# Softmax sums of four head pairs in one burst behind a projection, inverses spread through a DRAM scratch

## The chip, the cores and the metric

The kernel runs on one core of one Trainium2 chip. The metric is the device time of one execution in microseconds (us), the median of several runs. The core has five engines with a queue each: TensorE (PE in the profile, with its weight loads as PEld), VectorE (DVE), ScalarE (ACT), GpSimd (POOL) and SyncE (SP). Here POOL issues the loads, and SP the stores, the DMA transposes and the small copies inside the chip. Matrix products land in PSUM, which has eight banks of 128 partitions by 512 fp32; VectorE and ScalarE carry them on to SBUF.

## What is computed

A linear attention (keys and values are projected from 1024 positions to 64) followed by a two-layer network with a squared relu. There are 8 batches, 8 heads, 1024 positions and a head width of 64; the network goes from 512 to 2048 and back to 512.

```python
k_proj = np.einsum('ks,bhsd->bhkd', E, k)
v_proj = np.einsum('ks,bhsd->bhkd', F, v)
attn = np.exp(scale * np.matmul(q, k_proj.transpose(0, 1, 3, 2)))   # less the row maximum
attn = attn / (np.sum(attn, axis=-1, keepdims=True) + 1e-09)
x = np.matmul(attn, v_proj)         # heads side by side: 8192 tokens x 512
h = np.maximum(x @ w_in, 0.0)
out = h * h @ w_out
```

## The kernel before

**The network.** A batch is two chunks of 512 tokens. Both products of the network are done by a seven-product scheme on 2x2 blocks (sums and differences of blocks are formed on VectorE), so each has seven half-size products where eight would be plain. `Group` (lines 647 to 713) is the first product: a chunk has four groups, and a group has seven products p1, p5, p4 (of the group before), p6, p2, p3, p7, each of four matmuls of 256 columns (line 665). Their results are copied on ScalarE (L557, L690), passed through relu on ScalarE (L675) or added and passed through relu on VectorE (L679), and squared (L154). `second_spread` (line 590) is the second product, cut into quarters of four matmuls (L585). Its results leave through `put` (L575 on ScalarE or L154 on VectorE, then the store L579); `keep` (L557) puts a partial result aside in one of five buffers named "u".

**The order of the work.** TensorE's order is written out by hand. From the second batch on, the loop `both()` goes step by step: one product of the first layer and one quarter of the second, eight matmuls in all. A batch has 56 steps. The attention of a later batch is put between steps: `at(step, ...)` and `on(step, batch, name)` enter it in a plan. In the loop that fills the plan, t = 56(b-1)+28 is counted for batch b, and the attention entered is that of batches b+1 and b+2. The other engines' orders are made by a scheduler from the dependencies; SP and POOL take their transfers in order, so one that waits holds back those behind it.

**The attention of one batch.** `project` (L270, L271) projects all heads of K and V in 16 matmuls of 512 columns, two at a time, into the pair of banks that the attention has (one pair from the second batch on): K into the lower 64 partitions of the first bank, V into the upper 64 of the second. The other halves stay free. `keep_k` (L258, L259) and `keep_v` (L263, L264) copy them out. DMA transposes make kT (L304) and qT (L331). `scores` (L339) takes one pair of heads, and `exponentials` (L353) its Exp, into one of four buffers. `sums_spread` (L392) takes two pairs of heads: eight matmuls with a stationary operand of ones, 64 rows by 32 columns each, sum the exponentials over keys, each sum repeated on 32 partitions. Ln (L396) and Exp with scale -1 (L397) on 128x1024 make the inverse, and eight copies from SBUF to SBUF on SP (L403) spread it to the 64 rows of each head, 128 KB each. `values` (L415) multiplies with V, and VectorE (L419) multiplies by the inverse.

At the end, `second_seven` (line 624) is the second product of the last chunk. Its last product is accumulated in one bank, and its two halves leave by ScalarE (L575) and VectorE (L573) on two queues.

Of the kernel before, what the change touches and what calls it, by code (L numbers as in the profile page):

```python
# [1 line left out]

# [7 lines left out]
P = 128  # L10
F32 = mybir.dt.float32
BF16 = mybir.dt.bfloat16
AF = mybir.ActivationFunctionType
# [6 lines left out]
def kernel(  # L20
# [11 lines left out]
    nc = tc.nc  # L32
# [31 lines left out]
    part_pool = ctx.enter_context(tc.tile_pool(name="part", bufs=5))  # L64
    out_pool = ctx.enter_context(tc.tile_pool(name="outp", bufs=3))
    psum = ctx.enter_context(tc.tile_pool(name="ps", bufs=1, space=bass.MemoryType.PSUM))
    turn = {"att": 0, "bank": 0, "step": 1, "pairs": 2}

    lent = ctx.enter_context(ExitStack())
# [5 lines left out]
    def att_psum(shape=(P, 2, TCH), dtype=F32):  # L75
        turn["att"] += 1
        return pair_psum(turn["att"] % turn["pairs"], shape, dtype)

    def bank(shape=(P, 512), dtype=F32, n=None):
        if n is None:  # L80
            turn["bank"] += turn["step"]
            n = turn["bank"]
        return psum.tile(list(shape), dtype, tag=f"bank{n % 4}", name="ps_bank")
# [111 lines left out]
    def w_out_form(n, fb):  # L195
        if n in (1, 2, 3):
            return w_out_blk(fb + (0 if n == 1 else HF))[:, HM if n == 3 else 0:DM if n == 3 else HM]
        return w_out_sum[:, {5: 0, 6: 1, 7: 2, 4: 3}[n], fb]
# [28 lines left out]
    for h in half:  # L227
        nc.scalar.copy(kp[:, h].rearrange("p h a d -> p (h a d)"), zeros[:])
    kT = const_pool.tile([P, H, 2, KP], BF16, name="kT")
    VALUE_QUADS = ((LO, 0, 0, LO), (HI, 1, 1, HI), (HI, 0, 1, LO), (LO, 1, 0, HI))  # L230

    class Attention:
# [30 lines left out]
            nc.scalar.copy(self.vp[HI], view)  # L263
            nc.vector.tensor_copy(self.vp[LO], view)  # L264

        def project(self):
            ps = att_psum()
            for i in range(NI):
                f, l = i == 0, i == NI - 1
                nc.tensor.matmul(ps[LO, 0], lhsT=ET[:, i, :], rhs=self.K[:, :, i, :], start=f, stop=l)  # L270
                nc.tensor.matmul(ps[HI, 1], lhsT=FT[:, i, :], rhs=self.V[:, :, i, :], start=f, stop=l)  # L271
            self.keep_k(ps[LO, 0], slice(0, H))
            self.keep_v(ps[HI, 1])

        def project_k(self, g):
            ps = bank()
# [50 lines left out]
                    )  # L327
            nc.vector.tensor_copy(self.qT[:, 2 * pr:2 * pr + 2], ps[:])

        def transpose_q_dma(self):  # L330
            nc.sync.dma_start_transpose(  # L331
                self.qT[:].rearrange("p h n t -> p (h n) t"), self.Q[:].rearrange("p h i d -> p (h i d)")
            )


        def scores_mm(self, ps, pr, n):
# [46 lines left out]
                    nc.vector.tensor_copy(rs[j][lack:lack + 32], rs[j][have:have + 32])  # L383
                self.rs[pr + j] = rs[j]

        def sums_spread(self, pr):

            ps = att_psum()
            for j in range(2):
                for o, par, a, r in VALUE_QUADS:  # L390
                    c = 32 * (2 * a + j)
                    nc.tensor.matmul(  # L392
                        ps[c:c + 32, par], lhsT=ones[r, 0:32], rhs=self.e[pr + j][r, a], start=True, stop=True
                    )
            inv = soft_pool.tile([P, 2, TCH], F32, tag="rs", name="inv")
            nc.scalar.activation(inv[:], ps[:], AF.Ln)  # L396
            nc.scalar.activation(inv[:], inv[:], AF.Exp, scale=-1.0)  # L397
            for j in range(2):
                rs = soft_pool.tile([P, 2, TCH], F32, tag="rs", name="rs")
                for a in range(2):  # L400
                    have = 32 * (2 * a + j)
                    for to in (64 * a, 64 * a + 32):
                        nc.sync.dma_start(rs[to:to + 32], inv[have:have + 32])  # L403
                self.rs[pr + j] = rs

        def values(self, pr, spare=False):

# [40 lines left out]
    class Chunk:  # L448
# [104 lines left out]


        def keep(self, ps):
            u = part_pool.tile([P, DM], F32, name="u")
            nc.scalar.copy(u[:], ps)  # L557
            return u

        def half_product(self, n, i, ps, fresh=False):  # L560
            for fb in range(HF):
                nc.tensor.matmul(  # L562
                    ps[:, i * HM:(i + 1) * HM], lhsT=self.h_form(n, fb)[:, i * P:(i + 1) * P],
                    rhs=w_out_form(n, fb), start=fresh and i == 0 and fb == 0, stop=fb == HF - 1,
                    skip_group_check=True,
                )

        def put(self, a, mh, ps, more=None, part=None):
            o = out_pool.tile([P, 2, HM], F32, name="o_sb")
            n = slice(0, 2) if part is None else slice(part, part + 1)  # L570
            ps = ps.rearrange("p (i m) -> p i m", i=2)[:, n]
            if part:
                nc.vector.tensor_copy(o[:, n], ps)  # L573
            elif more is None:
                nc.scalar.copy(o[:, n], ps)  # L575
            else:
                tt(o[:, n], ps, ALU.add, more.rearrange("p (i m) -> p i m", i=2)[:, n])
            i = 4 * self.c + a + 2 * n.start
            (nc.scalar if part == 0 else nc.sync).dma_start(  # L579
                out_tokens[self.b][:, i:i + 2 * (n.stop - n.start) - 1:2, mh * HM:(mh + 1) * HM], o[:, n]  # L580
            )

# [38 lines left out]
            self.put(1, 0, chain)  # L621
            yield

        def second_seven(self, first, chain, other, last=False):
            def product(n, ps, fresh=False):
                self.half_product(n, 0, ps, fresh)
                yield
                self.half_product(n, 1, ps, fresh)

            yield from product(1, first, True)  # L630
            nc.scalar.copy(chain, first)
            yield
            yield from product(5, other, True)
            p5 = self.keep(other)
            yield
            yield from product(6, chain)
            u2 = self.keep(chain)
            yield
            yield from product(2, first)
            self.put(0, 0, first)  # L640
            yield
            yield from product(7, chain)
            self.put(1, 1, chain, p5)
            yield
            yield from product(3, other)
            self.put(0, 1, other, u2)
            yield
            yield from product(4, chain)
            if last:
                self.put(1, 0, chain, part=0)  # L650
                self.put(1, 0, chain, part=1)
            else:
                self.put(1, 0, chain)
            yield

    class Group:

# [63 lines left out]
    with tc.manual_schedule(engines={PE}):  # L721
# [33 lines left out]
        def at(step, fn, *args, **kwargs):  # L755
            plan.setdefault(step, []).append(lambda: fn(*args, **kwargs))

        def run(steps, start=0):
            for step, _ in enumerate(steps, start + 1):
                for stage in plan.pop(step, []):  # L760
                    stage()
            return step
# [62 lines left out]
        def second_bank(n):  # L825
            return second_pool.tile([P, 512], F32, tag=f"second{n}", name="ps_second")
# [40 lines left out]
        def on(step, b, name, *args):  # L867
            at(step, lambda: getattr(atts[b], name)(*args))
# [2 lines left out]
        on(6, 1, "chunk_values", 1, 0)  # L871
        on(12, 1, "chunk_sums", 1, 1)
        on(15, 1, "chunk_values", 1, 1)
        for b in range(B - 1):
            t = 56 * (b - 1) + 28
            if b:
                on(t + 1, b + 1, "scores", 3)
                on(t + 3, b + 1, "sums_spread", 2)
                on(t + 7, b + 1, "values", 0)
                on(t + 10, b + 1, "values", 1)  # L880
                on(t + 20, b + 1, "values", 2)
                on(t + 23, b + 1, "values", 3)
                at(t + 24, lambda b=b: chunk[b + 1, 0].sum_x())
            at(t + 51, lambda b=b: chunk[b + 1, 1].sum_x())
            if b + 2 < B:
                if b:
                    on(t + 11, b + 2, "load_q", lambda b=b: atts[b + 1].done)
                on(t + (26 if b else 32), b + 2, "transpose_q_dma")
                on(t + (28 if b else 36), b + 2, "project")
                on(t + (30 if b else 37), b + 2, "transpose_k_dma")  # L890
                if b + 3 < B:
                    at(t + (32 if b else 37), begin, b + 3)
                    on(t + (32 if b else 37), b + 3, "load_kv", lambda b=b: atts[b + 2].kT_done)
                on(t + (44 if b else 45), b + 2, "scores", 0)
                on(t + (47 if b else 48), b + 2, "scores", 1)
                on(t + (50 if b else 51), b + 2, "sums_spread", 0)
                on(t + (53 if b else 54), b + 2, "scores", 2)
        steps = both()
        run(steps)
        assert not plan, plan  # L900
        run(chunk[B - 1, 1].second_seven(second_bank(0)[:], second_bank(1)[:], bank(n=turn["bank"] + 1)[:], True))


# [28 lines left out]
```

The softmax here doesn't subtract the row's maximum and nothing guards it: scores larger than these inputs give would overflow.

## Time and profile before

| | |
|---|---|
| median of 3 runs | 474.89 us (473.21, 474.89, 474.94) |
| the profiled execution: its time | 473.25 us |
| its span, first to last instruction | 471.5 us |
| granted TensorE clock | 1.000 |
| one batch in the middle (163.15 to 218.50 us) | 55.35 us |
| ScalarE busy in it | 35.60 us |
| VectorE busy in it | 42.98 us |
| transfers `rs<-inv` | 96 of 128 KB, 2.3 us to landing (2.2 to 7.6) |

The profile is of one execution. Busy time of an engine is the time in which an instruction of it runs; matmuls are pipelined and their ends are modelled, so durations of neighbours overlap and starts are the better measure. A row of the timeline gives start, duration, engine, line, operation, tiles, form, how many were merged, and in brackets the idle time ahead and what ended it. A row of the groups gives the number of instructions, then busy time and mean ns of one, then idle time ahead of them.

### The profile page before, as it was taken

What the parts mean: (1) busy time and instruction counts of PE and PEld (TensorE: products, weight loads), DVE (VectorE), ACT (ScalarE), POOL (GpSimd) and SP (SyncE); (2) the same over time, 40 slices, a digit from 0 to 9 for tenths busy, and PEclk for the clock granted to TensorE, in tenths of its full rate; (3) what the DMA queues carried; (4) which work ended last, traced back from release to release, by engine and by line L of the source; (5) the groups of instructions that cost most, each with busy time, mean ns of one, the idle gap of its engine ahead of it and who ended that gap; (6) DMA issues with size and microseconds to landing.
All of it is one profiled execution on the core that took longest, in us unless ns stands there. A gap on an engine that the chain in (4) does not pass through costs nothing.

```text
span 471.5 us, 10107 instructions
## 1 busy us (share of the span) xinstructions
PE 464.1 (98%) x4123; PEld 367.6 (78%) x4141; DVE 347.6 (74%) x595; ACT 297.5 (63%) x484; POOL 34.0 (7%) x47
## 2 busy tenths in 40 slices
PE   8999999999999999999999999999999999999996
PEld 4544677888788787887888888888878878888885
DVE  2469985776968779567895779787796679968571
ACT  4488585887467864677457774568636875555641
POOL 7430100100010000100001000100000000000000
PEclk9999999999999999999999999999999999999999
DMA  9999999895869578785969749695692154101012
GB/s 182 201 205 207 158 206 203 166 217 106 186 138 207 137 141 195 133 171 131 170 180 153 170 98 183 153 197 147 116 219 71 39 132 100 68 24 68 24 69 89
DMA packets 85743, 67.90 MB, mean 144 GB/s; under 512 B 34368, under 2 KB 82240, under 8 KB 85696
## 3 DMA queue, kind: packets, MB, share of 16 engines
q0 software_dynamic: 32208, 29.23, 40.6%
q1 hardware_dynamic: 53344, 37.89, 30.1%
q8 instruction: 32, 0.52, 0.4%
q10 hardware_dynamic: 144, 0.13, 0.1%
q14 instruction: 15, 0.12, 0.1%
HBM read 59.24 MB, written 16.78 MB: 161 GB/s over the span
## 4 chain that ended last, share of the span: by engine, by line
PE 97%; DMA 1%; DVE 1%; ACT 1%; issue 0%; SPq 0%; ACTq 0%; DVEq 0%
PE ps_bank L665 38%; PE ps_second L585 36%; PE ps_bank L502 6%; PE ps_bank L562 3%; PE ps_att L270 3%; PE ps_att L339 2%; PE ps_second L562 2%; PE ps_att L415 2%; DMA k_f<-in_k_dram 1%; PE ps_att L392 1%; PE ps_bank L314 1%; PE ps_att L349 1%; PE ps_att L345 1%; PE ps_bank L220 0%; PE ps_att L289 0%; PE ps_bank L278 0%
## 5 line engine op out<-in xcount | busy, mean ns | idle before, releaser
L154 DVE TENSOR_TENSOR h<-h 128x1024 bf16<-128x1024 bf16 (+1 forms) x170 | 105.4, 645 | 43.9 <-ACT h L675 38.7
L665 PE MATMUL ps_bank<-x_sum,w_in_sum 128*128 128x256 bf16 x672 | 101.1, 273 | 0.1
L665 PEld LDWEIGHTS <-w_in_sum 128*128 128x128 bf16 x896 | 85.5, 98 | 18.9 <-issue 6.3
L585 PEld LDWEIGHTS <-h 128*128 128x128 bf16 x896 | 87.6, 98 | 10.7
L679 DVE CUSTOM_DVE_ANT_0 h<-ps_bank,u 128x512 bf16<-128x512 f32 x112 | 73.8, 685 | 16.2 <-PE ps_bank L665 12.1
L557 ACT COPY u<-ps_bank 128x512 f32<-128x512 f32 x115 | 68.0, 591 | 24.9 <-PE ps_bank L665 23.7
L690 ACT COPY ps_bank<-ps_bank 128x512 f32<-128x512 f32 x56 | 32.0, 571 | 81.5 <-PE ps_bank L665 81.5
L675 ACT ACTIVATE h<-ps_bank 128x512 bf16<-128x512 f32 x112 | 67.9, 607 | 16.7 <-PE ps_bank L665 15.8
L665 PEld LDWEIGHTS <-w_in 128*128 128x128 bf16 x672 | 64.3, 98 | 14.5 <-issue 5.2
L585 PEld LDWEIGHTS <-s 128*128 128x128 bf16 x672 | 65.7, 98 | 7.6
L665 PE MATMUL ps_bank<-xT,w_in 128*128 128x256 bf16 x448 | 67.3, 273 | 0.3
L585 PE MATMUL ps_second<-w_out_sum,s 128*128 128x256 bf16 x448 | 67.2, 273 | 0.0
L585 PE MATMUL ps_second<-w_out_sum,h 128*128 128x256 bf16 x448 | 67.0, 273 | 0.0
L585 PE MATMUL ps_second<-w_out,h 128*128 128x256 bf16 x448 | 64.7, 272 | 0.0
L419 DVE TENSOR_TENSOR xT<-ps_att,rs 128x512 bf16<-128x512 f32 x48 | 30.9, 685 | 13.7 <-PE ps_att L415 13.7
L353 ACT ACTIVATE expT<-ps_att 128x1024 bf16<-128x1024 f32 x32 | 33.1, 1034 | 5.2 <-PE ps_att L339 3.4
L665 PE MATMUL ps_bank<-x_sum,w_in 128*128 128x256 bf16 x224 | 33.7, 273 | 0.3
L665 PE MATMUL ps_bank<-xT,w_in_sum 128*128 128x256 bf16 x224 | 33.6, 273 | 0.1
L154 DVE TENSOR_TENSOR o_sb<-ps_second,u 128x512 f32<-128x512 f32 x29 | 19.9, 685 | 18.7 <-PE ps_second L585 13.6
L585 PE MATMUL ps_second<-w_out,s 128*128 128x256 bf16 x224 | 33.6, 273 | 0.0
L502 PE MATMUL ps_bank<-xT,w_in 128*128 128x512 bf16 x124 | 28.8, 379 | 0.4 <-issue 0.2
L154 DVE TENSOR_TENSOR s<-h 128x1024 bf16<-128x1024 bf16 x32 | 22.0, 691 | 3.7 <-PE ps_second L585 3.0
(97 smaller groups left out, 453.4 us busy)
## 6 DMA issues: line engine op xcount, KB each, us to landing
out_dram<-o_sb SPq DMA_DIRECT2D x63, 256.0 KB, 2.5
rs<-inv SPq DMA_DIRECT2D x96, 128.0 KB, 2.3
K_sb<-in_k_dram POOLq DMA_DIRECT2D x7, 1024.0 KB, 10.2
V_sb<-in_v_dram POOLq DMA_DIRECT2D x7, 1024.0 KB, 14.5
Q_sb<-in_q_dram POOLq DMA_DIRECT2D x6, 1024.0 KB, 11.8
w_out<-in_moe_w_out_dram POOLq DMA_DIRECT2D x4, 512.0 KB, 15.8
Q_sb<-in_q_dram POOLq DMA_DIRECT2D x4, 256.0 KB, 11.0
V_sb<-in_v_dram POOLq DMA_DIRECT2D x2, 512.0 KB, 10.8
```

What stands on the lines that cost most here:

```text
L154: return nc.vector.tensor_tensor(out=o, in0=x, in1=y, op=op)
L270: nc.tensor.matmul(ps[LO, 0], lhsT=ET[:, i, :], rhs=self.K[:, :, i, :], start=f, stop=l)
L353: self.done = nc.scalar.activation(e[:], ps[:], AF.Exp, scale=SCALE)
L419: self.done = nc.vector.tensor_tensor(out=self.xT[:, pr, :, par], in0=ps_x[par].rearrange("p (c t) -> p c t", c=2), in1=rs[:, par].rearran ...
L502: nc.tensor.matmul(ps[:], lhsT=w_in_blk(cb, fb), rhs=self.xT[:, cb, self.c].rearrange("p a t -> p (a t)"), start=(cb == 0), stop=(cb == NC ...
L557: nc.scalar.copy(u[:], ps)
L562: nc.tensor.matmul(ps[:, i * HM:(i + 1) * HM], lhsT=self.h_form(n, fb)[:, i * P:(i + 1) * P], rhs=w_out_form(n, fb), start=fresh and i == ...
L585: nc.tensor.matmul(ps[:, i * HM:(i + 1) * HM], lhsT=self.h_form(n, fb)[:, i * P:(i + 1) * P], rhs=w_out_form(n, fb), start=fresh and i == ...
L665: nc.tensor.matmul(ps[:, j * HC:(j + 1) * HC], lhsT=w_in_form(n, cb, 2 * self.g + j), rhs=self.chunk.x_form(n, cb), start=fresh and j == 0 ...
L675: nc.scalar.activation(self.out(kh, a), ps[:], AF.Relu)
L679: nc.vector._custom_dve(TENSOR_ADD_SAT, out=self.out(kh, a), in0=ps[:], in1=more[:], s0=3.0e38, s1=0.0)
L690: nc.scalar.copy(self.chain[:], self.first[:])
```

## The change

The sums of all four head pairs of a batch are taken in one burst of 16 matmuls. The stationary operand is a new constant `pick`: for pair m, its columns 8m to 8m+7 are ones and the rest zeros, so the four pairs accumulate into one tile of 32 partitions with eight rows each. They go to the half of the attention's two banks that the projection leaves free: in batches 3 to 6 `project` of the batch after runs first and the sums behind it, in batches 2 and 7 the sums run alone. There are one Ln for each bank on 64 partitions, and one Exp on 128x512. The inverses go to a DRAM scratch in two writes. `spread` reads a pair's rows back, each repeated eight times, in two transfers of 64 partitions by 4 KB. Batch 1 keeps its own way.

The plan moves with it. Scores of batch b+2 go from t+44 to t+57 to t+29, +36, +40, +44. Its projection, with the sums of the batch before, goes to ten steps ahead of the next t, with the kT transpose and the spreads of pairs 0 to 2 a step later and the qT transpose behind them. Values go from t+7, +10, +20, +23 to t+7, +11, +17, +21, and pair 3 is spread behind the first of them. Q is loaded from t+12, K and V from t+18. Batches 2 and 3 have steps of their own. In the last chunk the two halves of the last product get a bank each, and each is added on VectorE to a kept partial result and stored by SP.

```diff
+    dram_pool = ctx.enter_context(tc.tile_pool(name="inv_dram", bufs=2, space=bass.MemoryType.DRAM))
...
+    pick = const_pool.tile([P, H // 2, 32], BF16, name="pick")
+    nc.scalar.copy(pick[:].rearrange("p m k -> p (m k)"), zeros[:, 0:P])
+    for m in range(H // 2):
+        nc.scalar.copy(pick[:, m, 8 * m:8 * m + 8], ones[:, 0:8])
...
-        def project(self):
+        def project(self, sums=None):
             ps = att_psum()
...
+            if sums:
+                sums.sums_all(ps)
+                sums.log(1)
             self.keep_k(ps[LO, 0], slice(0, H))
             self.keep_v(ps[HI, 1])
+            if sums:
+                sums.log(0)
+                sums.inverse_all()
...
-        def sums_spread(self, pr):
-
-            ps = att_psum()
-            for j in range(2):
+        def sums_all(self, ps=None):
+            ps = att_psum() if ps is None else ps
+            for m in range(H // 2):
                 for o, par, a, r in VALUE_QUADS:
-                    c = 32 * (2 * a + j)
+                    c = HI.start * (1 - par) + 32 * a
                     nc.tensor.matmul(
-                        ps[c:c + 32, par], lhsT=ones[r, 0:32], rhs=self.e[pr + j][r, a], start=True, stop=True
+                        ps[c:c + 32, par], lhsT=pick[r, m], rhs=self.e[m][r, a],
+                        start=m == 0, stop=m == H // 2 - 1, skip_group_check=True,
                     )
...
+        def log(self, par):
+            rows = (HI, LO)[par]
+            nc.scalar.activation(self.inv[rows], self.ps_sums[rows, par], AF.Ln)
+
+        def inverse_all(self):
+            nc.scalar.activation(self.inv[:], self.inv[:], AF.Exp, scale=-1.0)
+            self.inv_dram = dram_pool.tile([2, H // 2, 8, 2, TCH], F32, name="inv_dram")
+            for par in range(2):
+                nc.sync.dma_start(
+                    self.inv_dram[:, :, :, par].rearrange("a p i t -> (a p i) t"), self.inv[(HI, LO)[par]]
+                )
+
+        def spread(self, pr, behind=None):
+            rs = soft_pool.tile([P, 2, TCH], F32, tag="rs", name="rs")
+            for a, rows in enumerate((LO, HI)):
+                row = self.inv_dram[a, pr].rearrange("i b t -> i (b t)")
+                with tc.issue_after(behind.ins) if behind else nullcontext():
+                    self.spread_done = nc.sync.dma_start(
+                        rs[rows].rearrange("p b t -> p (b t)"), row.unsqueeze(0).broadcast_to((8, 8, 2 * TCH))
+                    )
+            self.rs[pr] = rs
...
-            yield from product(4, chain)
-            if last:
-                self.put(1, 0, chain, part=0)
-                self.put(1, 0, chain, part=1)
+            if ends:
+                o = out_pool.tile([P, 2, HM], F32, name="o_sb")
+                for i, ps in enumerate(ends):
+                    self.half_product(4, i, ps, True)
+                    self.put(1, 0, ps, u3, i, o)
+                    yield
             else:
+                yield from product(4, chain)
                 self.put(1, 0, chain)
...
+        on(8, 2, "project")
+        for pr in range(4):
+            on((18, 20, 22, 24)[pr], 2, "scores", pr)
+            if pr < 3:
+                on(27, 2, "spread", pr)
+        plan[27].insert(0, lambda: atts[2].sums_alone())
+        on(42, 3, "project")
...
+                    at(t - 10, lambda b=b: atts[b + 2].project(atts[b + 1]))
+                    on(t - 9, b + 2, "transpose_k_dma")
+                else:
+                    on(t - 10, b + 1, "sums_alone")
+                for pr in range(3):
+                    on(t - 9, b + 1, "spread", pr)
```

## The prediction, made before the changed kernel ran

> **What bounds the kernel now.** I read the page's head, then the windows of equal stages, then TensorE's timeline inside one of them, because a share of 98% says that TensorE is the bound but not whether it ever waits.
>
> ```profile
> span 471.5 us, 10107 instructions
> PE 464.1 (98%) x4123; PEld 367.6 (78%) x4141; DVE 347.6 (74%) x595; ACT 297.5 (63%) x484; POOL 34.0 (7%) x47
> ...
> PE 97%; DMA 1%; DVE 1%; ACT 1%; issue 0%; SPq 0%; ACTq 0%; DVEq 0%
> ```
>
> The chain that ended last is TensorE almost from end to end. By windows, the 7.4 us in which it is idle lie in the first 20 us (2.64) and after 454 us (3.7). One batch in the middle has 0.1:
>
> ```profile
> 163.15:218.50 55.35, 55.25 (x505) 45.54 (x505) 42.98 (x72) 35.60 (x60) 2.62 (x3) 1.00 0.76 158
> ```
>
> (Length, then busy time of PE, PEld, DVE, ACT, POOL, then clock, DMA share, GB/s.) So work taken from ScalarE or the queues is worth nothing by itself here. What counts is what TensorE executes, and waits that are new. TensorE's timeline prices the parts:
>
> ```profile
> 33.26 1.03 PE L502 MATMUL ps_bank<-xT,w_in 128*128 128x512 bf16 x4
> 34.22 0.41 PE L349 MATMUL ps_att<-expT,vp 64*64 64x256 bf16 x8
> 34.56 0.61 PE L502 MATMUL ps_bank<-xT,w_in 128*128 128x512 bf16 x2
> ```
>
> ```profile
> 183.58 0.60 PE L585 MATMUL ps_second<-w_out_sum,h 128*128 128x256 bf16 x4
> 184.11 0.40 PE L270 MATMUL ps_att<-K_sb,ET 128*64 128x512 bf16 x1
> ...
> 185.65 0.38 PE L271 MATMUL ps_att<-V_sb,FT 128*64 128x512 bf16 x1
> 185.96 0.61 PE L665 MATMUL ps_bank<-xT,w_in 128*128 128x256 bf16 x4
> ...
> 205.66 0.60 PE L585 MATMUL ps_second<-w_out,s 128*128 128x256 bf16 x4
> 206.19 0.41 PE L392 MATMUL ps_att<-expT,ones 64*32 64x512 bf16 x8
> 206.53 0.61 PE L665 MATMUL ps_bank<-x_sum,w_in_sum 128*128 128x256 bf16 x4
> ```
>
> Read starts, not durations: four feed-forward matmuls of 256 columns go by in 0.437 us, so a step (four of the first layer, four of the second) is 0.874. An inserted burst costs the start-to-start time less that: the eight sums matmuls 206.53 - 205.66 - 0.44 = 0.43, the projection 185.96 - 183.58 - 0.44 = 1.94. A batch of 56 steps, projection, and two sums, four scores and four values bursts of 0.43 makes 48.9 + 1.94 + 4.3 = 55.2 against 55.35 seen: nothing else is in it.
>
> **What the skill says.** "TensorEngine Tiling (Array Packing)", Tiling Modes: the array splits into eight 64x32 tiles that work independently, and changing the mode drains it. The trace agrees: the eight sums matmuls start together, one round of 512 columns is 0.215 (from 184.11 to 185.65 are seven projection rounds), and the other 0.21 of the 0.43 is the two changes of mode. "DMA: Bandwidth & Descriptors", Anatomy of one DMA, puts a fixed cost of about 2 us on a transfer, worst where HBM is written. The trace has 2.3 for `rs<-inv` inside SBUF, and no HBM scratch. Same page, Queues, rings and completion order: an engine takes turns between queues by packets. The trace shows what a loaded turn costs, below.
>
> **The change, part by part.**
>
> *Sums on TensorE.* Before: two bursts a batch, each on all eight 64x32 tiles, 2 x 0.43 = 0.86. After: 16 matmuls as well, but a head pair uses four tiles, and the next pair accumulates onto the same four. So they are four rounds in series: 4 x 0.215 = 0.86 of streaming. That rounds on the same tiles queue is shown by L349 above: eight matmuls of 256 columns on four tiles cost 34.56 - 33.26 - 0.87 = 0.43, like four of 512. Batches 2 and 7 run them alone: 0.86 + 0.21 = 1.07, which is +0.21 each. Batches 3 to 6 run them behind a projection, and pay between nothing and 0.2 for one more change of mode; I take one drain, +0.1 each. Sum: 0.42 + 0.4 = **+0.8** (0.4 to 1.2).
>
> *ScalarE.* Before, Ln and Exp twice a batch:
>
> ```profile
> L397 ACT ACTIVATE inv<-inv 128x1024 f32<-128x1024 f32 x12 | 12.7, 1062 | 0.2
> L396 ACT ACTIVATE inv<-ps_att 128x1024 f32<-128x1024 f32 x12 | 12.3, 1023 | 1.2 <-PE ps_att L392 1.2
> ```
>
> That is 4.2 us. After: two Ln on 64x512 and one Exp on 128x512, each near the 0.58 of the 64x512 vp cast (L263), 1.8 in all. The 2.4 us freed are worth **0**: TensorE waited for none of them. The five small fills of `pick` stand in ScalarE's idle 2.68 us ahead of the first K cast (5.85 us): 0; without that cover at most five times the 0.57 of a kp fill, 2.9.
>
> *The next user of the attention PSUM pair.* There is one pair. The projection now holds it longer (Ln, two kp copies of 0.68, vp, Ln), but values follow 17 steps (15 us) later. Behind ScalarE's vp copy, which now waits for the kp copies, stand a relu and a chain copy with about 1 us to spare. The tightest new pair is scores of group 3, then the projection two steps later: from the end of the p5 product the Exp can start at 0.93 and ends at 1.96, the projection comes at 2.62. Slack 0.6; cost 0, up to 0.6 in each of five batches. The dense scores of batch 2 (every second step) leave 0.5 or more each: 0. `inv` takes one of five "u" buffers until its two writes land, and the next user of that buffer comes some ten ScalarE instructions (about 9 us) later: 0.
>
> *SP and POOL.* SP issues 10 transfers a batch in place of 16 (5.9 us of issue for 9.4); 2.25 MB for 2. Order on SP: kT transpose, a store, two scratch writes, a store, six spreads, qT transpose (4 us), a store, two spreads. The stores behind have three buffers and come four steps apart or more: 0. In a later batch the spread of pair 0 should land some 12 us after its projection, and values come after 15. K and V are issued at step t+18 behind Q at t+12, and are needed at t+46: 32 us for 25 (Q 11 and K with V 14.4). 0.
>
> *Batch 2 is different:* its spread meets the loads of batch 3.
>
> ```profile
> rs<-inv SPq DMA_DIRECT2D x96, 128.0 KB, 2.3
> ```
> ```profile
> rs<-inv SPq DMA_DIRECT2D x4, 128.0 KB, 6.4
> ```
> ```profile
> K_sb<-in_k_dram POOLq DMA_DIRECT2D x1, 1024.0 KB, 8.6
> V_sb<-in_v_dram POOLq DMA_DIRECT2D x1, 1024.0 KB, 14.4
> ```
>
> First line: all of them. Second: the four issued at 113.9 to 116 us, with a Q load under way. Last: K and V issued from 86 us. Today the first values of batch 2 start at 108.6 (step 35); in the new plan at step 37, 108.64 + 1.75 + 0.21 = 110.6, and the second at 113.65. The sums end ten steps before, at 101.9; Ln, Ln, Exp to 103.7; two writes issued by 105.0. Q of batch 3 is now loaded ahead of K and V, so V lands about 14.4 - 8.6 = 5.8 later, near 108, and the writes land with it. Two spreads issued by 109.2, landing 1.8 to 3 later, two multiplications of 0.685: 112.4 to 113.6. That is just in time. VectorE stands at that multiplication meanwhile, with a square and two relu sums behind it. Bounds 0 to 6; I take **+0.5**, once.
>
> *Tail.*
>
> ```profile
> 467.88 0.37 ACT L575 COPY o_sb<-ps_second 128x256 f32<-128x256 f32 x1 [4.70 <-PE ps_second L562]
> 468.28 0.38 ACTq L579 DMA_DIRECT2D out_dram<-o_sb  x1
> 468.28 0.42 DVE L573 COPY o_sb<-ps_second 128x256 f32<-128x256 f32 x1 [1.50 <-ACT o_sb L575]
> ```
>
> VectorE's half waits for ScalarE's, since both read one bank; its store is the last. With a bank each, the first half leaves during the second half's matmuls, and one VectorE addition (about the 0.42 of the copy) follows the last matmul: **-0.4** (-0.2 to -0.5).
>
> *Sum:* 0.8 + 0.5 - 0.4 = +0.9. On the profiled execution's own time, 473.25, that is 474.15. The three runs have a median of 474.89 (473.21, 474.89, 474.94), so the profiled one is a low one; on the median it is 475.8. I take the middle, 475.0.
>
> **Rivals.** (B) The batch 2 spread is late: if V of batch 3 lands past 111.5, both hops are caught. Writes 105.0 + 6.4 = 111.4, spreads 1.2 of issue and 5.8, multiplication 1.4: 119.8, and TensorE stands at the second values from 113.65: 6.1 in place of 0.5, 480.6. For it: the 6.4 in the trace. Against: Q, K and V should be in by 108. It decides from 2.4 us of lateness. (C) The four rounds overlap as the eight tiles do now: 6 x 0.43 = 2.6 less, no late spread, 471.9. Against: L349. (D) ScalarE is one 0.6 us copy late for the projection in each of five batches: +3.0, 478.0. Against: today scores of group 3 and sums are two steps apart as well, and TensorE does not wait there.
>
> **Chances.** A, as summed, 55%, 475.0 (472.8 to 477.2); B 25%; C 8%; D 12%. This kernel's measurement can tell about 0.5% (2.4 us) from no change. Faster: most of C and a little of A, 0.06. Slower: most of B, over half of D, a little of A, 0.33. Same: 0.61. The range, 472.8 to 480.5, leaves out most of C below and half of B above, some 2 in 10.
>
> **What would show it.** Right: the projection with sums costs 2.9 us from start to start, the sums alone about 1.07; the batches last 55.4 to 55.6; ScalarE about 14 us less busy with no gain in span; after the last matmul one VectorE addition of about 0.4. Wrong: gaps of TensorE ahead of values or a projection (B: at 113 to 120 us, VectorE waiting for a DMA `rs<-inv_dram`; D: at each projection), or sums whose 16 matmuls take 0.65 (C).

## The result, and the profile after

The changed kernel takes **497.0 us** (median of four runs, 495.27 to 499.9), the kernel before, in runs beside it, 474.91 (473.21 to 475.49). The ratio is 1.048, with a 95% interval from 1.043 to 1.052: 22 us slower, and far outside the forecast range of 472.8 to 480.5. The profiled execution took 496.92 us, of which the span is 495.1.

First the head of the page, the clock and the chain that ended last, for the kernel after.

```profile
span 495.1 us, 10023 instructions
PE 470.1 (95%) x4118; PEld 370.7 (75%) x4141; DVE 348.6 (70%) x596; ACT 287.0 (58%) x483; POOL 34.0 (7%) x47
...
PEclk9999999997979999999999999999999999999999
...
PE 59%; DMA 22%; DVE 10%; ACT 3%; SPq 2%; issue 2%; DVEq 0%; POOLq 0%
```

The chain was TensorE for 97%; now it is TensorE for 59%, and DMA and VectorE hold 32%. The clock line, all nines in a TensorE that never rests, has two sevens, in the slices of 12.4 us that begin at 111 and 136 us. TensorE is busy for 6.0 us longer than before, and the span is 23.6 longer, so most of the loss is time in which it stands. Who makes it stand is in the groups (busy, mean ns of one, idle time before and what ended it) and in the waits (total, times, longest), both of the kernel after:

```profile
L454 DVE TENSOR_TENSOR xT<-ps_att,rs 128x512 bf16<-128x512 f32 x48 | 31.3, 685 | 42.0 <-DMA rs<-inv_dram 35.8
```

```profile
DVE xT L454 <- DMA rs<-inv_dram: 35.8, 13, 5.3
...
PE ps_bank L704 <- DVE h L718: 7.6, 7, 2.1
...
PE ps_att L352 <- DMA kT<-kp: 5.1, 1, 5.1
...
PE ps_att L450 <- DVE xT L454: 3.4, 5, 1.9
```

VectorE stood 35.8 us, in 13 places, at the multiplication of the values by the inverses (L454), for the spread that brings these inverses. TensorE's waits follow from it: for the next values, because `xT`'s multiplication frees their PSUM, and for a bank (L704), because the relu sum (L718) that empties it stands behind that multiplication on VectorE. The third is a separate one: once, for 5.1 us, TensorE waits for the transposed keys `kT`.

The place and the size of the loss come from the start of the same feed-forward weight load in both traces. The changed kernel is 0.6 us late at the load that the kernel before starts at 21 us, 16.4 late at the one that it starts at 169 us, in batch 3, then 2.0, 1.5, 3.5 and 0.5 more in the next four batches: 23.9, less 0.2 at the tail. So two thirds are lost between batch 2 and batch 3, and some 2 us in each later batch. The first stop, on VectorE and then on TensorE:

```profile
114.86 1.29 DVE L454 TENSOR_TENSOR xT<-ps_att,rs 128x512 bf16<-128x512 f32 x2 [5.26 <-DMA rs<-inv_dram]
116.20 0.41 PE L450 MATMUL ps_att<-expT,vp 64*64 64x512 bf16 x4 [1.88 <-DVE xT L454]
```

Windows of 2 us of TensorE alone (length, PE busy, clock, DMA share, GB/s) show what lies in that stretch:

```profile
114.00:116.00 2.00, 0.32 (x3) 1.00 0.51 123
116.00:118.00 2.00, 1.80 (x15) 0.85 0.51 123
118.00:120.00 2.00, 1.35 (x7) 0.50 0.54 129
120.00:122.00 2.00, 1.56 (x8) 0.50 0.48 117
122.00:124.00 2.00, 2.00 (x11) 0.50 1.02 201
138.00:140.00 2.00, 0.73 (x7) 1.00 1.21 195
140.00:142.00 2.00, 0.00 (x0) 0.83 1.22 196
142.00:144.00 2.00, 0.21 (x1) 0.50 1.19 216
144.00:146.00 2.00, 1.78 (x8) 0.50 1.17 246
146.00:148.00 2.00, 2.00 (x11) 0.50 1.17 245
```

Two things are to be seen. From 117.4 us, behind the first stop, and from 141.3 us, within the second, the clock is 0.50 for 6.8 us, so that a stop costs more than its idle time: a projection round takes 0.43 us from start to start at 120.44, where it takes 0.215 otherwise. And in the first stop the DMA engines are **half busy**, at 117 to 129 GB/s, though VectorE waits for a spread. They are not crowded by loads: the last load ahead of it landed at 107.3 us.

What SP has issued meanwhile, in the timeline of its queue (start, time that the issue took):

```profile
108.08 3.86 SPq L430 DMA_DIRECT2D rs<-inv_dram  x6
112.04 12.42 SPq L344 DMA_TRANSPOSE qT<-Q_sb  x1
124.56 0.53 SPq L612 DMA_DIRECT2D out_dram<-o_sb  x1
125.20 1.24 SPq L430 DMA_DIRECT2D rs<-inv_dram  x2
126.53 4.99 SPq L316 DMA_TRANSPOSE kT<-kp  x1
```

Six spreads, then the transpose of the next queries, whose issue holds SP for 12.4 us; before it held SP for 4.0. Behind it stand the spread of pair 3 and then `kT`. K of batch 4 was issued at 124.36, two microseconds ahead of `kT`, with Q and V next to it, and they landed at 139.6, 146.7 and 153.6; TensorE's wait for `kT` ends at 143.8.

A later batch has only the first half of that. VectorE's timeline in batch 3:

```profile
181.04 1.29 DVE L454 TENSOR_TENSOR xT<-ps_att,rs 128x512 bf16<-128x512 f32 x2 [0.49 <-DMA rs<-inv_dram]
186.31 1.29 DVE L454 TENSOR_TENSOR xT<-ps_att,rs 128x512 bf16<-128x512 f32 x2 [3.98 <-DMA rs<-inv_dram]
...
199.01 1.29 DVE L454 TENSOR_TENSOR xT<-ps_att,rs 128x512 bf16<-128x512 f32 x2 [2.09 <-DMA rs<-inv_dram]
```

Pair 0 comes 0.5 late, pair 1 4.0 late, pair 3 2.1 late. And the DMA view of 171 to 193 us, in 40 slices, for the same batch:

```profile
DMA  5719894014564549954555445464545907999999
GB/s 205 272 48 212 201 320 171 0 60 179 141 156 104 134 119 208 159 119 127 119 149 119 134 104 149 104 164 104 134 119 110 85 25 154 290 290 290 290 290 378
```

From the tenth slice (176 us) to the thirty-first (188) the engines are half busy at about 119 GB/s; this is the six spreads. Then comes the queries' transpose, all busy, at 290. A pair is two transfers of 256 KB, 524 KB: at 119 GB/s that is 4.4 us, and VectorE's two multiplications start 5.3 apart. In the prediction a spread had a landing time of 1.8 to 3 us and no throughput.

### The profile page after: what moved, and what is told of

Same layout as the page of the kernel before. It is cut to its first block, busy times and chain, and to the rows that moved or that the text cites. A ratio compares the mean times of both kernels' runs of the same rounds, so it can differ in the third digit from the quotient of the medians.

```text
span 495.1 us, 10023 instructions
## 1 busy us (share of the span) xinstructions
PE 470.1 (95%) x4118; PEld 370.7 (75%) x4141; DVE 348.6 (70%) x596; ACT 287.0 (58%) x483; POOL 34.0 (7%) x47
## 3 DMA queue, kind: packets, MB, share of 16 engines
HBM read 71.83 MB, written 18.35 MB: 182 GB/s over the span
## 4 chain that ended last, share of the span: by engine, by line
PE 59%; DMA 22%; DVE 10%; ACT 3%; SPq 2%; issue 2%; DVEq 0%; POOLq 0%
PE ps_bank L704 20%; PE ps_second L618 19%; DMA rs<-inv_dram 15%; PE ps_bank L537 6%; PE ps_bank L597 4%; DMA kT<-kp 3%; PE ps_att L276 3%; DMA inv_dram<-inv 3%; DVE xT L454 2%; PE ps_att L352 2%; SPq L430 2%; DVE h L155 2%; DVE h L718 2%; PE ps_second L597 1%; DMA K_sb<-in_k_dram 1%
## 5 line engine op out<-in xcount | busy, mean ns | idle before, releaser
L704 PE MATMUL ps_bank<-x_sum,w_in_sum 128*128 128x256 bf16 x672 | 101.8, 274 | 7.8 <-DVE h L718 7.6
L704 PEld LDWEIGHTS <-w_in_sum 128*128 128x128 bf16 x896 | 87.1, 98 | 25.4 <-issue 12.0
L718 DVE CUSTOM_DVE_ANT_0 h<-ps_bank,u 128x512 bf16<-128x512 f32 x112 | 73.0, 684 | 7.2 <-ACT h L714 3.5
L704 PEld LDWEIGHTS <-w_in 128*128 128x128 bf16 x672 | 64.1, 98 | 15.6 <-issue 7.0
L704 PE MATMUL ps_bank<-xT,w_in 128*128 128x256 bf16 x448 | 67.5, 273 | 0.1
L454 DVE TENSOR_TENSOR xT<-ps_att,rs 128x512 bf16<-128x512 f32 x48 | 31.3, 685 | 42.0 <-DMA rs<-inv_dram 35.8
L704 PE MATMUL ps_bank<-x_sum,w_in 128*128 128x256 bf16 x224 | 34.1, 275 | 0.3
L704 PE MATMUL ps_bank<-xT,w_in_sum 128*128 128x256 bf16 x224 | 33.6, 273 | 0.0
```

The lines of the kernel that those rows point to most:

```text
L454: self.done = nc.vector.tensor_tensor(out=self.xT[:, pr, :, par], in0=ps_x[par].rearrange("p (c t) -> p c t", c=2), in1=rs[:, par].rearran ...
L704: nc.tensor.matmul(ps[:, j * HC:(j + 1) * HC], lhsT=w_in_form(n, cb, 2 * self.g + j), rhs=self.chunk.x_form(n, cb), start=fresh and j == 0 ...
L718: nc.vector._custom_dve(TENSOR_ADD_SAT, out=self.out(kh, a), in0=ps[:], in1=more[:], s0=3.0e38, s1=0.0)
```

## The experiments

The theory after this reading: the spreads stream at half rate because each is read with an outermost dimension of eight; all else (VectorE at L454, SP behind the transpose, `kT` into the loads) follows. The rivals are that the place of the queries' transpose in SP's queue makes them late, that loads of later batches do, or that it is the new plan and the new sums rather than the transfers. All ratios are to the kernel before, in runs beside the experiment's.

### Sixteen engines for the same bytes

```
-    rs[rows]..., row.unsqueeze(0).broadcast_to((8, 8, 2 * TCH))
+    rs[rows]..., row[0:4].unsqueeze(0).broadcast_to((16, 4, 2 * TCH))
```

As many transfers, bytes and plan steps as in the kernel after, but each half is filled with sixteen copies of four rows in place of eight copies of eight. Nothing is lost by it: `pick` has eight columns of ones for a pair, so the eight rows of a pair are equal, and four of them hold all that is needed. This kernel, and the one of the experiment with both mends, computes what the kernel after computes.

> The spread reads four of a pair's eight equal rows and repeats them 16 times, in place of eight rows eight times: same bytes, same count. Theory S (the scratch reads run on half of the 16 DMA engines, about 4.3 us for the two transfers of a pair, and that makes spreads late and holds the qT transpose on SP for 12 us): a pair lands in some 2.2 us, the qT transpose takes about half of its 12.9 us on SP, VectorE's waits for rs<-inv_dram fall from 35.8 us to under 12, and the time falls from 497 to 483 to 488. Rival H (the scratch in HBM is slow to read back whatever the engines): pairs take 4 us as before, the time stays at 495 to 498. Rival K (the loads of batch 4 ahead of the kT transpose make most of the loss): the time falls by 3 at most.

Measured: 477.2 us (476.84 to 478.04), ratio 1.006 (1.0036 to 1.0084). One access pattern brings back 20 of 22 us, more than was expected. The waits of this run, and its page's DMA issues (count, KB, median us to landing), span and bytes:

```profile
DVE xT L454 <- DMA rs<-inv_dram: 2.9, 1, 2.9
...
PE ps_att L352 <- DMA kT<-kp: 1.5, 1, 1.5
```

```profile
span 475.5 us, 10046 instructions
...
HBM read 71.83 MB, written 18.35 MB: 190 GB/s over the span
...
rs<-inv_dram SPq DMA_DIRECT2D x48, 256.0 KB, 4.3
```

The bytes are those of the kernel after (71.83 and 18.35 MB too). In batch 3 the three pairs of the burst land at 168.1, 171.6 and 172.9 us, and the DMA engines reach a mean of some 250 GB/s from 165 to 169 (the first line below, whose last two numbers are DMA share and GB/s). The records of the single packets say the same: of the 64 packets of 4 KB in a spread, eight are under way at a time in the kernel after, and a spread takes 2.1 us; here it is sixteen, and 1.0 to 1.1 us. One packet takes about as long in both (median 0.26 and 0.22 us). So what halves the rate is how many engines work at a time, not that eight rows are read in place of four. The issue of the queries' transpose holds SP for 6.5 us in place of 12.4, so its length was a consequence of the slow spreads ahead of it. The second line below is a whole batch, from projection to projection (length, then busy time of PE, PEld, DVE, ACT, POOL, clock, DMA share, GB/s):

```profile
165.00:169.00 4.00, 4.00 (x39) 3.55 (x38) 3.90 (x7) 3.13 (x6) 0.00 (x0) 1.00 0.90 249
...
152.04:207.44 55.40, 55.40 (x505) 45.80 (x505) 43.07 (x72) 33.48 (x59) 2.63 (x3) 1.00 0.78 162
```

The batch is 55.40 us with no idle time of TensorE, against 57.29 with 55.47 busy in the kernel after.

### The loads of batch 4 behind kT

```
-    on(44, 4, "load_kv")
+    on(44, 4, "load_kv", lambda: atts[3].kT_done)
```

> K and V of batch 4 are loaded behind the kT transpose of batch 3 in place of right behind its projection. Theory K: that transpose shares the DMA engines with 3 MB of loads and lands at 143.8, so TensorE stands 5.2 us at the first scores of batch 3 and then runs about 4 us at half clock (some 2 us more): the time falls by 6 to 8, to 489 to 491, and the wait of TensorE for kT<-kp goes. Theory S alone: the transpose is late because the spread of pair 3 and the qT transpose hold SP, so the wait only shrinks and the time falls by less than 3.

Measured: 489.0 (487.05 to 490.28), ratio 1.0303 (1.0269 to 1.0337), 8 us less than the kernel after. TensorE's wait for `kT` is gone. The spreads are as late in kind as before:

```profile
DVE xT L454 <- DMA rs<-inv_dram: 23.0, 9, 6.1
```

So the 5 us stop at 138 us, with the half clock behind it, was `kT` among the loads of the batch after, and is a third of the loss. It needs the late `kT` first: the transpose is issued at 126.5 because SP was held; in the first experiment it is issued at 121.0, beside the same loads, and TensorE waits 1.5 us for it.

### The queries' transpose ahead of the spreads

```
-    on(t - 9, b + 2, "transpose_q_dma", b + 1)
+    on(t - 9, b + 2, "transpose_q_dma")
-    on(28, 3, "transpose_q_dma", 2)
+    on(28, 3, "transpose_q_dma")
```

> The qT transpose isn't held behind the spreads of pairs 0 to 2 any more; it goes as soon as Q is there and qT is free. Theory S: its 12.9 us on SP are mostly time behind the spreads; ahead of them it takes 4 us as in the kernel before, pair 3 is spread some 10 us earlier, and the waits of VectorE for pair 3 go, but pairs 0 and 1 stay as late or come a little later: 490 to 494. Rival K: no change of the batch 3 wait from this, under 2 us in all. If the transpose takes 12 us wherever it stands, the theory of the queue behind it is wrong.

Measured: 508.31 (507.73 to 510.18), ratio 1.072 (1.0689 to 1.0751): worse than the kernel after, where a gain was expected. SP's timeline in batch 3:

```profile
161.89 3.95 SPq L344 DMA_TRANSPOSE qT<-Q_sb  x1
168.51 1.24 SPq L316 DMA_TRANSPOSE kT<-kp  x1
171.28 0.38 SPq L612 DMA_DIRECT2D out_dram<-o_sb  x1
172.32 1.15 SPq L421 DMA_DIRECT2D inv_dram<-inv  x2
173.56 0.53 SPq L612 DMA_DIRECT2D out_dram<-o_sb  x1
181.60 3.78 SPq L430 DMA_DIRECT2D rs<-inv_dram  x6
```

In the later batches the transpose takes 4 us again, as expected. But the spreads are issued 9.3 us after the scratch writes, where the kernel after has 3.0 (171.38 and 174.41). The transpose frees the Q buffer, and POOL, which waits only for a buffer, issues the next 1 MB load of Q at 169.6 us; in the kernel after the same load came at 195.3. The scratch writes run into it. TensorE then waits 4.0 to 4.4 us at the second values of three later batches.

Batch 2 has another cause besides. There the transpose starts while K and V of batch 3 are still on their way (they land at 102.9 and 109.4 us), and holds SP for 10.6 us:

```profile
99.86 10.57 SPq L344 DMA_TRANSPOSE qT<-Q_sb  x1
...
111.16 1.13 SPq L421 DMA_DIRECT2D inv_dram<-inv  x2
```

The scratch writes leave at 111.2, where the kernel after has 104.3, and the spreads behind them meet a load of Q issued at 114.6. TensorE waits 11.0 us at the second values.

### The same, with the load of Q held back

The last reading was tested by itself: the edit above, and in the later batches the load of Q behind the last spread.

```
-    on(t + 12, b + 3, "load_q")
+    on(t + 12, b + 3, "load_q", lambda b=b: atts[b + 1].spread_done)
```

> e3_qT_first with one edit more: in batches 4 to 7 the load of Q waits until the spread of pair 3 of the batch before has been issued and landed. Theory L (e3 was slower because the early qT transpose frees the Q buffer, so that POOL starts the next Q load at once, at 169.6 where it was 195.3, and the scratch writes at 172.3 land behind it): the waits of 4.2 to 4.6 us at the second values of three batches go, and of 508.3 some 494 to 497 is left, with the 11 us wait of batch 2, whose loads are not touched. If the transpose itself and not the load holds up the scratch writes: 506 to 510.

Measured: 492.47 (489.77 to 494.21), ratio 1.0392 (1.0361 to 1.0423): 16 us less than without the load held back. SP's timeline in the same batch:

```profile
171.67 1.15 SPq L421 DMA_DIRECT2D inv_dram<-inv  x2
172.92 0.53 SPq L612 DMA_DIRECT2D out_dram<-o_sb  x1
174.71 3.78 SPq L430 DMA_DIRECT2D rs<-inv_dram  x6
```

From write to spread it is 3.0 us again. So in the later batches the load made the difference. The stop in batch 2, whose loads this edit does not touch, stays (10.4 us in one wait): the transpose holds SP for 9.9 us there, and a load of Q is issued at 113.6.

Against the kernel after, the total (492.5 for 497.0) is therefore the sum of a loss and a gain. By the starts of the same weight loads, from 21 us to the load that the kernel before starts at 119 us this kernel loses 14.6 us (the kernel after 7.9), from there to 169 us 0.7 (7.9), and behind that 2.7 (7.5). So with slow spreads, the transpose ahead of them and the load held back together save some 12 us outside batch 2. In the first experiment the transpose stands where it does in the kernel after, and TensorE waits 1.5 us for `kT` and 0.3 for a bank: it is the slow spreads that make its place costly.

### The new plan with the old sums

The old `sums_spread`, two bursts a batch with the inverses spread inside SBUF, put into the new plan and tail:

```
-        plan[27].insert(0, lambda: atts[2].sums_alone())
+        on(27, 2, "sums_spread", 0)
+        on(31, 2, "sums_spread", 2)
...
-                    at(t - 10, lambda b=b: atts[b + 2].project(atts[b + 1]))
+                    on(t - 10, b + 2, "project")
...
+                on(t - 8, b + 1, "sums_spread", 0)
+                on(t + 3, b + 1, "sums_spread", 2)
...
-                    on(t - 9, b + 2, "transpose_q_dma", b + 1)
+                    on(t - 7, b + 2, "transpose_q_dma", b + 1)
```

> The new order of scores, projection, values and loads, and the new tail, but with the sums, inverses and SBUF-to-SBUF spreads of the kernel before (two bursts a batch, eight transfers of 128 KB each, no DRAM scratch). If the scratch and its spread make the loss (theory S), TensorE has no waits but the one for kT of batch 3 at most: 475 to 483. If the new order of work makes it (theory K, or ScalarE and VectorE being busy at the wrong steps), 489 to 497.

Measured: 482.03 (480.9 to 483.79), ratio 1.0158 (1.0119 to 1.0198). No wait of VectorE for a spread is left. But TensorE has new waits at the bursts that the experiment put in, which share one PSUM pair with their neighbours. Four times 1.2 us a burst two steps behind the projection waits until that is copied out, and once, in batch 2, values wait 3.0 us for a Ln:

```profile
PE ps_att L405 <- DVE vp L270: 4.7, 4, 1.2
PE ps_att L472 <- ACT inv L409: 3.0, 1, 3.0
```

The profiled execution has a span 9.6 us over that of before. These waits are 7.7 of it, and a half clock of 3.4 us behind the longest of them takes 1.7 more. So nothing of size is left for the plan, but it is no clean separation: where the bursts stand and the plan can't be read apart in it.

### Both mends together

The first two edits in one kernel.

> The edits of e1_read16 and e2_load_behind_kT together. Theory S with K (the reads on half the engines make most of the loss, the loads ahead of the kT transpose most of what e1 left): TensorE's 1.7 us wait for kT<-kp goes, what is left is 0.5 to 1 us more of sums on TensorE and a head some 1 us later, less 0.4 at the tail: 475 to 476.5, not to be told from the kernel before. If something else in the new order costs, 477 and more.

Measured: 475.88 us (six runs, 474.8 to 476.43) against 473.95, ratio 1.0046 (1.0029 to 1.0062), as expected. The span is 473.9, 2.4 us over that of before, and the starts of the same weight loads divide it: 1.4 is there at the first one (21 us), 1.2 is added up to the last matmul, and 0.2 is given back at the end. The first part can't be put down to the change: the next experiment has 1.9 there, with nothing ahead of it changed. So the change, mended, costs about what its sums cost on TensorE, and still gains nothing.

### The old kernel with the new tail

The diff's part in `second_seven`, `half_product` and `put` alone, on the kernel before.

> The kernel before with the new tail alone: the last product's halves in a bank each, added on VectorE to a kept partial result, both stored by SP. As predicted: 0.2 to 0.5 us less after the last matmul, 474.3 to 474.7, no change that can be told. If the two stores on one queue cost more than they save: 475 and more.

Measured: 474.16 us (22 runs, 472.56 to 476.25), ratio 1.0001 (0.999 to 1.0012). From the start of the last group of matmuls to the end of VectorE's last instruction it is 2.37 us (467.75 to 470.12) where before has 2.81 (465.89 to 468.70), so the tail itself is 0.44 shorter; the total doesn't show it. (The same 2.37 stands in every trace with the new tail.) In this run the first feed-forward weight load started 1.9 us later than in the profiled execution of before, though nothing ahead of it is changed: the head varies by that much by itself.

### The old kernel with a scratch that nobody reads

Two tiles of the DRAM scratch added to the kernel before and written once each in batches 6 and 7, since a scratch in DRAM is itself something that the kernel before did not have.

```
+            if self.b in (6, 7) and pr == 2:
+                scratch = dram_pool.tile([P, 2, TCH], F32, name="scratch")
+                nc.sync.dma_start(scratch[:], inv[:])
```

> The kernel before with two DRAM scratch tensors that two late extra writes of 512 KB fill and nothing reads. Asked: do the first feed-forward matmuls, which start 0.6 to 1.9 us later in the changed kernels with a scratch and not in the one without, come later because a scratch is there? If so: 475.3 to 476.5 and a start of 21.5 and more in place of 20.9 us. If the start varies by itself: 474.7 to 475.2, and a start that has nothing to do with it. The two writes themselves are expected to cost nothing.

Measured: 474.39 (14 runs, 473.36 to 476.2), ratio 1.001 (0.9996 to 1.0024), and the first weight load starts 0.14 us later. That a scratch is there costs nothing measurable.

## Why the prediction was wrong

**The step that failed** is "In a later batch the spread of pair 0 should land some 12 us after its projection, and values come after 15", which made the cost of late spreads 0, with its twin in batch 2, "Two spreads issued by 109.2, landing 1.8 to 3 later". Both price a spread as one transfer's time to landing, taken from transfers of 128 KB inside SBUF. They leave out that six of 256 KB in a row have a rate.

The issues came about when they should: the two transfers of pair 0 were issued by 109.5 us in batch 2, and by 10.3 us after the projection with its sums in batch 3 (165.42 to 175.71). But VectorE could multiply pair 0 only 5.4 and 5.3 us after that (114.86 and 181.04), and pair 1 another 4.2 to 5.6 us later in batches 2 to 6. In batch 3 that is 15.6 us after the projection for pair 0, not 12, where values come after 15.0 (180.39). With sixteen engines its second half lands 3.1 us after its issue and 13.2 after the projection (154.87 to 168.11), which still meets values at 15.0; another 2 us don't.

The rate could have been read from the diff. "DMA: Bandwidth & Descriptors", Rules for kernel authors, says that an outermost dimension below 16, a leading broadcast of c copies as its example, confines a transfer to at most c engines. The added line has `broadcast_to((8, 8, ...))`. The trace agrees: eight packets at a time, a share of one half and about 119 GB/s, against sixteen packets and some 250 GB/s with sixteen copies of four rows.

By its other steps:

- *The bound*: TensorE, with nothing to gain from other engines' time. Right. ScalarE became 10.5 us less busy (forecast: about 14), and no run showed a gain from that.
- *Sums on TensorE*: right. The projection with its sums costs 2.92 us (162.06 to 165.42, less the 0.44 of the group ahead of it), forecast 2.9; alone, 102.33 - 100.82 - 0.44 = 1.07, forecast 1.07. A batch where nothing is late is 55.40, forecast 55.4 to 55.6. The term of 0.8 is therefore sound; with small waits of 0.5 (0.32 for a bank, 0.18 at a projection) it is about the 1.2 that both mends leave.
- *Batch 2, 0.5*: wrong by its size. TensorE stood 1.9 us at the second values and 1.1 at the projection behind them, and lost 2.6 more to the half clock (two groups of four that start 0.86 apart for 0.44, eight projection rounds of 0.43 for 0.215).
- *ScalarE and the PSUM pair (D)*: right that it costs nothing. With both mends TensorE has no wait for ScalarE at a projection.
- *SP, "qT transpose (4 us)"*: wrong. It was moved behind six spreads and took 12.4 to 13.0 us to issue, which delayed pair 3 in batches 2 to 6 and `kT` in batch 3.
- *K and V, "32 us for 25": 0*: right for K and V themselves. What was not asked is what their loads run into: the issue of the first of them has no place in the plan's time, it comes when a buffer is free, and here that was 2 us ahead of `kT`.
- *Tail, -0.4*: the trace has -0.44, the total can't show it.
- *Rivals*: C is out (the 16 matmuls take 1.07 alone). B named the right place, batch 2 with VectorE at the multiplication, but gave it the loads as its cause, and so confined it to one batch. K, V and Q of batch 3 were in by 107.3 us, seven before the first stop, and DMA is half idle in it.

The 15.8 us that are lost from 21 us to the load that the kernel before starts at 169 us can be divided roughly. TensorE's stops are 8.6 (1.9, 1.1, 0.3, 5.1 and 0.2), and about 10 us of work at half clock lost some 5. The kernel with both mends, in which nothing of size waits, is 2.9 late at the same load and 1.2 at the end, so some of the rest is only that the new plan does work earlier. What stays open is how the 7.5 us of the later batches divide, and why the issue of a transpose takes longer behind slow spreads or beside loads: that it does is measured, the mechanism isn't.

## What to carry to other kernels

When a small transfer is replaced by a burst of larger ones, price the burst by bytes over the rate that its access pattern allows, and look first at the outermost dimension of both sides. Where the rows that are repeated are equal, as here, that dimension is free to choose. Then read what stands behind it in the same queue, because a slow burst also lengthens the issue of the next transfer and so moves transfers that have nothing to do with it. A step number in a plan orders work, but a load leaves when its buffer is free: moving the last reader of a buffer moves a load.

## What was not expected of the hardware

- The 0.50 clock came behind a stop of only 1.9 us and a busy stretch of 1.2 (117.4 to 124.2 us), as well as within one of 5.1, 2.6 us after TensorE's last matmul had ended (141.3 to 148.1). "TensorE: Matmul & The Clock Gate", Part 1, gives an idle window of about 3.4 us. Here less was enough.
- The issue of the same DMA transpose held SP for 3.9 to 4.2 us in the kernel before, 6.5 to 7.6 behind six spreads on sixteen engines, 12.4 to 13.0 behind the same on eight, and 9.9 to 10.6 in batch 2 of the third and fourth experiments, beside loads of K and V.
- Scratch writes of 128 KB landed 2.3 to 3.3 us after their issue in the run with sixteen engines; with a 1 MB load of Q under way, the spreads that wait for them were issued 9.3 us after them in place of 3.0.
